# Attention, a dense MLP and a routed MoE on one core: the SP transfer queue follows the written table, and the zero fill of the result becomes eighteen transfers in the first pass

## The chip, the core and the metric

The kernel runs on one core of a Trainium2 chip. The core has a matrix engine (TensorE, PE in the profile), three more compute engines (VectorE or DVE, ScalarE or ACT, GpSimd or POOL) and SyncE (SP), which here only issues transfers. Each engine works through its own list of instructions in order and waits on semaphores; the transfers themselves run on sixteen DMA engines. The metric is the device time of one execution in microseconds (us); of several executions the median is taken.

## The reference

Three layers in float32 precision, one after the other:

```python
# 1 attention: 4 batches x 8 heads, 576 positions, head size 64, window 128
scores = q @ k.T / 8;  scores += -slope[h] * |i - j|  where 0 <= i - j < 128, else -1e9
x = softmax(scores) @ v                       # 2304 tokens x 512
# 2 dense MLP, 512 -> 2048 -> 512
x = (relu(x @ w_in) ** 2) @ w_out
# 3 mixture of experts: 8 experts, 512 -> 1024 -> 512, two per token
noisy = x @ w_gate + log1p(exp(x @ w_noise)) * noise
top2  = two largest per token, weights = softmax over the two
out   = zeros(2304, 512)
for e in range(8): out[mask] += weight * (relu(x[mask] @ w1[e]) @ w2[e])
```

The result starts as zeros because each expert adds its rows to it.

## The kernel before

**Tiling.** The 2304 tokens are 18 tiles of 128. Attention works tile by tile (tile i needs the keys and values of tiles i-1 and i), the dense MLP on 9 groups g of two tiles, with the hidden layer cut into 16 chunks f. To keep float32 precision every operand of a product is split into a high and a low part, and three products are summed (`mm1`, `mm2`, lines 284 to 295).

**Stages.** First pass, to about 160 us: the attention of tiles 0 to 5 and the MLP of groups 0 to 2, while the 32 half chunks of the MLP's weights are loaded and unpacked. From then on one group after the other (groups 3 to 8, some 60 us each), each beside the attention of the next two tiles and the gate of an earlier group. From about 525 us on the experts' weights are loaded, and the experts run to the end; their rows are gathered from the scratch tensor `yd` in HBM and the results scattered into the output.

**What sets the order.** A table `ORDER` of some 1900 steps is written out by hand. A step is a name and indices and calls one small function. The names used below:

- `LQ.i` and `LK.i` load the 512 KB tile `qks` (queries and keys of tile i, line 366), `LV.i` the 256 KB tile `vs` (values, line 370). `LVx` is a second load of the values of tile 5.
- `KH.i`, `KL.i`, `Q1.i`, `QH.i`, `QL.i` scale and split queries and keys (`kth`, `ktl`, `qh`, `ql`); `KHx`, `KLx` do it once more for tile 5. From tile 6 on `Q1` and `QL` run on POOL.
- `AV.i` multiplies probabilities (`pv`, `pc`) with the values of tiles i-1 and i (line 511).
- `H.g.f`, `E1.g.f`, `E2.g.f`, `GL.g.f`, `Y.g.f` are one chunk of the dense MLP: first product (line 290), relu, square and high part on ACT (lines 538, 544, 545), low part on DVE (line 550), second product (line 295).
- `WL.h` loads half chunk h of the MLP's weights (512 KB, line 250); `WA.h` is its first use, on ACT (line 258), and further steps unpack it.
- `YA.g`, `YB.g` copy a finished group to `ysb` and store it in `yd` (line 570); `G5.g` stores the gate weights of a group (`g_wd`, line 664); `TABA`, `TABP`, `TABC` build the experts' token tables (DVE lines 702 to 705 make `r_a` and `r_b`, PE line 713 multiplies them).
- `EL.k` loads chunk k of the experts' weights (`wst`, line 217), `EA.k` and `EB.k` split it.

The table holds for PE, ACT, DVE and POOL. SP is not in the set: its transfers are put in an order by the scheduler of the framework, which takes each when it reckons that it becomes ready.

**Buffers around the change.** From tile 6 on there is one `qks` buffer, so `LQ.6` needs `KLx` done with it, and two `vs` buffers, so `LV.i` needs `AV.(i-1)` done. In the first pass `kth` has seven slots; slot 0 stands for the keys before tile 0, is set to zero once and stays zero.

**The zero fill.** `consts_late` (line 319) runs when the first pass is over. It loads the gate's weights and noise (`wg`, `nz`), clears a tile (line 337) and writes it to all 18 tiles of the result in one transfer (line 338).

Of the kernel before, what the change touches and what calls it, by code (L numbers as in the profile page):

```python
# [50 lines left out]
Y.0.11 WR.27 GL.1.10 E1.2.4 WC.27 E2.2.4 Y.1.10 WB.28 WL.30 WA.29 H.0.12 GL.2.4 WR.28 WG.29 WC.28 Y.2.4 E1.0.12
E2.0.12 WB.29 H.1.11 WL.31 WA.30 GL.0.12 WR.29 WG.30 Y.0.12 E1.1.11 WC.29 E2.1.11 H.2.5 GL.1.11 WB.30 Y.1.11
WA.31 E1.2.5 WG.31 E2.2.5 H.0.13 WR.30 GL.2.5 WC.30 Y.2.5 E1.0.13 WB.31 E2.0.13 H.1.12 GL.0.13 WR.31 WC.31
Y.0.13 E1.1.12 LK.5 E2.1.12 LV.6 H.2.6 LVx.5 GL.1.12 Y.1.12 E1.2.6 E2.2.6 H.0.14 GL.2.6 KHx KLx Y.2.6 E1.0.14
LQ.6 E2.0.14 H.1.13 GL.0.14 Y.0.14 E1.1.13 E2.1.13 H.2.7 Q1.6 KH.6 GL.1.13 KL.6 QH.6 Y.1.13 E1.2.7 QL.6 E2.2.7
# [15 lines left out]
NM.9.1 TY.1.1 XH.8 GL.3.13 H.3.15 QH.10 M.9.0 TYC.1.1 QL.10 E1.3.14 XL.8 TP.9.1 E2.3.14 RANK.0 YB.2 LOG.1 LQ.11
M.9.1 Y.3.13 RANKC.0 AV.9 LOGC.1 GL.3.14 E1.3.15 TABA.0.0 E2.3.15 Q1.11 FOLD.1 LV.10 Y.3.14 XH.9 G1.1 GL.3.15
A1.1 XL.9 TABP.0.0 G2.1 Y.3.15 A2.1 TABA.0.1 H.4.0 TABC.0.0 G3.1 TABP.0.1 H.4.1 E1.4.0 TABC.0.1 E2.4.0 G4.1
H.4.2 GL.4.0 A4.1 Y.4.0 E1.4.1 G5.1 E2.4.1 RANK.1 H.4.3 GL.4.1 E1.4.2 RANKC.1 E2.4.2 Y.4.1 TABA.1.0 H.4.4 GL.4.2
E1.4.3 E2.4.3 Y.4.2 GL.4.3 E1.4.4 E2.4.4 TABP.1.0 Y.4.3 TABA.1.1 H.4.5 GL.4.4 TABC.1.0 TABP.1.1 Y.4.4 E1.4.5
# [5 lines left out]
E1.4.12 E2.4.12 Y.4.11 G5.2 C0.11.1 GL.4.12 EX.11.0 C1.11.1 RANK.2 H.4.13 MX.11.1 KH.12 RS.11.0 Y.4.12 QH.12
RANKC.2 NM.11.0 EX.11.1 H.4.14 TABA.2.0 E1.4.13 E2.4.13 AV.10 RS.11.1 KL.12 NM.11.1 GL.4.13 E1.4.14 QL.12
E2.4.14 TP.11.0 LV.11 TP.11.1 XH.10 GL.4.14 TABP.2.0 LQ.13 M.11.0 Y.4.13 M.11.1 H.4.15 TABA.2.1 AV.11 E1.4.15
E2.4.15 XL.10 Q1.13 TABC.2.0 TABP.2.1 GL.4.15 LV.12 Y.4.14 XH.11 TABC.2.1 XL.11 Y.4.15 H.5.0 H.5.1 E1.5.0 E2.5.0
H.5.2 GL.5.0 E1.5.1 E2.5.1 Y.5.0 GL.5.1 E1.5.2 E2.5.2 Y.5.1 GL.5.2 H.5.3 Y.5.2 E1.5.3 E2.5.3 H.5.4 GL.5.3 Y.5.3
# [1009 lines left out]
```

## Time and profile before

| | before |
|---|---|
| median of 3 runs | 1049.85 us (1049.78 to 1050.63) |
| the profiled execution | 1050.41 us |
| its span, first to last instruction | 1048.6 us |
| mean granted TensorE clock | 0.984 of full speed |
| PE busy | 992.9 us, 95% of the span |
| DVE, ACT, POOL busy | 577.2, 508.5, 245.7 us (55%, 48%, 23%) |
| moved by DMA | 103.40 MB, mean 99 GB/s |

The span is what the profile's rows speak of; the execution's time is 1.8 us longer. PE is busy nearly throughout, so what counts is the idle time in front of its matmuls, and the stretches in which its clock was granted at half speed.

### The profile page before, as it was taken

To read this page: it belongs to the slowest core of one execution; us is meant where nothing else is said; L and a number is where in the kernel's file an instruction comes from. 1 tells how busy PE (TensorE), PEld (TensorE's weight loads), DVE (VectorE), ACT (ScalarE), POOL (GpSimd) and SP (SyncE) were. 2 spreads that over 40 slices of the span, in tenths; PEclk is the share of its full clock that TensorE was granted. 3 is DMA by queue.
4 is the path that set the end of the run, shared out by engine and by line. 5 is a ranking of instruction groups with operands and counts; after the bars stand their busy time and mean duration, and the time that the engine had idled before them with its cause. 6 is when DMAs were issued, how large, how long until landed. Compare 5 with 4: busy or idle time off the path is not lost.

```text
span 1048.6 us, 17826 instructions
## 1 busy us (share of the span) xinstructions
PE 992.9 (95%) x6636; PEld 870.2 (83%) x6636; DVE 577.2 (55%) x1693; ACT 508.5 (48%) x1245; POOL 245.7 (23%) x220
## 2 busy tenths in 40 slices
...
GB/s 280 59 142 103 167 81 260 42 71 22 51 13 31 41 42 41 41 42 13 20 102 152 167 71 228 137 116 177 90 170 117 170 95 170 123 88 68 46 47 48
DMA packets 36234, 103.40 MB, mean 99 GB/s; under 512 B 7495, under 2 KB 7751, under 8 KB 36144
## 3 DMA queue, kind: packets, MB, share of 16 engines
...
HBM read 85.24 MB, written 20.00 MB: 100 GB/s over the span
## 4 chain that ended last, share of the span: by engine, by line
PE 66%; DVE 14%; DMA 8%; issue 5%; ACT 4%; POOL 2%; SPq 1%; POOLq 0%; DVEq 0%; ACTq 0%
PE h L290 30%; PE y L295 29%; DMA old<-out_dram,idx 4%; PE y L421 2%; PE y L511 2%; DMA qks<-in_qk_dram 2%; PE y L798 1%; DVE sb L447 1%; ACT sb L459 1%; DVE gl L550 1%; DMA vs<-in_v_dram 1%; DVE w L280 1%; DVE sb L438 1%; PE y L490 1%; DVE pc L498 1%
## 5 line engine op out<-in xcount | busy, mean ns | idle before, releaser
L290 PE MATMUL h<-xh,w 128*128 128x256 f32 x1152 | 229.7, 285 | 0.0
L290 PE MATMUL h<-xeh,w 128*128 128x304 f32 (+2 forms) x1024 | 229.2, 305 | 0.0
L295 PE MATMUL y<-w,gh 128*128 128x512 f32 x576 | 186.6, 405 | 8.2 <-ACT gh L545 8.2
L290 PEld LDWEIGHTS h<-xh,w 128*128 128x128 f32 x1152 | 187.8, 191 | 7.0 <-issue 1.2
L295 PE MATMUL y<-w,hh 128*128 128x512 f32 (+1 forms) x584 | 182.6, 394 | 0.0
L290 PEld LDWEIGHTS h<-xeh,w 128*128 128x128 f32 x1024 | 171.5, 188 | 2.9 <-issue 0.4
L290 PE MATMUL h<-xl,w 128*128 128x256 f32 x576 | 163.1, 283 | 1.1 <-DVE xl L527 1.0
L290 PE MATMUL h<-xel,w 128*128 128x304 f32 (+2 forms) x512 | 154.8, 302 | 0.3 <-DVE wt L815 0.3
L226 DVE TENSOR_TENSOR w<-wst,w 128x1024 fp32r<-128x1024 f32 x64 | 78.4, 1225 | 138.2 <-ACT w L222 131.6
L550 DVE TENSOR_TENSOR gl<-r,gh 128x256 fp32r<-128x256 f32 x144 | 68.4, 475 | 123.1 <-ACT gh L545 122.9
L222 ACT ACTIVATE w<-wst 128x1024 fp32r<-128x1024 f32 x64 | 67.7, 1058 | 127.9 <-PE y L295 113.0
L295 PEld LDWEIGHTS y<-w,gh 128*128 128x128 f32 x576 | 99.9, 190 | 27.5 <-ACT gh L545 8.4
L295 PEld LDWEIGHTS y<-w,hh 128*128 128x128 f32 (+1 forms) x584 | 103.2, 182 | 21.8
L538 ACT ACTIVATE r<-h 128x256 f32<-128x256 f32 x144 | 54.8, 381 | 136.5 <-PE h L290 96.8
L838 ACT ACTIVATE hh<-h 128x304 fp32r<-128x304 f32 (+1 forms) x118 | 49.7, 421 | 141.5 <-PE h L290 138.0
L295 PE MATMUL y<-w,gl 128*128 128x512 f32 x288 | 114.3, 397 | 1.5 <-DVE gl L550 1.4
L290 PEld LDWEIGHTS h<-xl,w 128*128 128x128 f32 x576 | 110.1, 191 | 5.8 <-DVE xl L527 1.9
L295 PE MATMUL y<-w,hl 128*128 128x512 f32 (+1 forms) x292 | 114.9, 394 | 0.0
L843 DVE SCALAR_TENSOR_TENSOR hl<-h,hh 128x304 fp32r<-128x304 f32 (+1 forms) x118 | 55.0, 467 | 98.2 <-ACT hh L838 91.5
L774 POOL DMA_INDIRECT xg<-yd,idx x40 | 42.4, 1060 | 258.6 <-PE h L290 92.1
L290 PEld LDWEIGHTS h<-xel,w 128*128 128x128 f32 x512 | 96.4, 188 | 2.0 <-DVE wt L815 0.5
L264 POOL TENSOR_SCALAR wsg<-wa 128x512 f32<-128x512 f32 x32 | 54.9, 1717 | 65.3 <-ACT wa L258 52.3
(180 smaller groups left out, 1478.0 us busy)
## 6 DMA issues: line engine op xcount, KB each, us to landing
wst<-in_w_exp_dram SPq DMA_DIRECT2D x64, 512.0 KB, 3.6
w<-in_w_moe_dram SPq DMA_DIRECT2D x32, 512.0 KB, 3.7
qks<-in_qk_dram SPq DMA_DIRECT2D x19, 512.0 KB, 3.6
...
out_dram<-ysb SPq DMA_DIRECT2D x1, 4608.0 KB, 15.3
...
xg<-yd,idx POOLq DMA_INDIRECT x40
out_dram<-old,idx POOLq DMA_INDIRECT x29
```

Source lines behind the costliest of these rows:

```text
L222: nc.scalar.activation(w[:, 0], st, AF.Copy)
L226: nc.vector.tensor_tensor(out=w[:, 1], in0=st, in1=w[:, 0].bitcast(F32), op=OP.subtract)
L264: nc.gpsimd.tensor_scalar(sg.bitcast(F32), a.bitcast(F32), 0.0, None, op0=OP.mult)
L290: nc.tensor.matmul(ps, w[:, wi, c], x[:, kk, :], start=(n == 0), stop=(n == 3 * KD - 1))
L295: nc.tensor.matmul(ps, g, w[:, wi, DM:], start=(start and n == 0), stop=(stop and n == 2))
L421: nc.tensor.matmul(sp[c][:, pp], a[r, p, :], b[r, p, s0:s0 + 2, :], start=(n == 0), stop=(n == 2))
L511: nc.tensor.matmul(o[64 * c:64 * c + 64, 2 * hf + pp, :], vv[n][:, 4 * hf + j, :], pts[n][:, j, :], start=(n == 0), stop=(n == 1))
L538: nc.scalar.activation(r, HT.pop((g, f)), AF.Relu)
L550: nc.vector.tensor_tensor(out=gl, in0=r, in1=gh.bitcast(F32), op=OP.subtract)
L774: nc.gpsimd.indirect_dma_start(out=xg, out_offset=None, in_=yd[:rows, :], in_offset=col(e, t), bounds_check=rows - 1, oob_is_err=False)
L838: nc.scalar.activation(HH[e, f, part][0][:, c0:c1], HP[e, f, part][j], AF.Relu)
L843: nc.vector.scalar_tensor_tensor(out=hl, in0=HP[e, f, part][j], scalar=0.0, in1=hh.bitcast(F32), op0=OP.max, op1=OP.subtract)
```

## The change

1. SP joins the set of engines that follow the table. Its transfers are issued in the order of the steps.
2. The single zero fill is gone, with the tile that it was copied from and that tile's clear on DVE. A new step `ZF.t` writes one tile of 128 rows of the result (256 KB) from slot 0 of `kth`. That slot is four runs of 128 floats in each partition, so one step writes 512 runs of 512 bytes. The table has eighteen: four after `WL.5`, four after `WL.6`, and one after each of `WL.7` to `WL.16`.
3. The loads of `wg` and `nz` become a step `LR`, after `LQ.6`.
4. The copies of the token weights of experts 0 and 1 (`wt`) need no longer keep the written place. On DVE they stay where they were.

PE, ACT and POOL have the same instructions in the same order as before, DVE too but for the clear that is gone. The diff (of the table one line of each):

```diff
-EX.0.1 RS.0.0 MX.1.0 NM.0.0 LQ.5 KH.4 MX.1.1 EX.1.0 RS.0.1 WC.0 TP.0.0 EX.1.1 WB.2 S.2.0 RS.1.0 WG.3 WL.5 C0.2.0
+NM.0.0 LQ.5 KH.4 MX.1.1 EX.1.0 RS.0.1 WC.0 TP.0.0 EX.1.1 WB.2 S.2.0 RS.1.0 WG.3 WL.5 ZF.3 ZF.2 ZF.1 ZF.0 C0.2.0
...
         nc.vector.memset(runcum, 0.0)
+
+    def l_rout():
         nc.sync.dma_start(out=wg.rearrange("p k e -> p (k e)"), in_=w_gate)
         nc.sync.dma_start(out=nz.rearrange("p t e -> p (t e)"), in_=noise)
-        z = gp.tile([P, DM], F32, name="ysb", bufs=2)
-        nc.vector.memset(z, 0.0)
-        nc.sync.dma_start(out=out.rearrange("(t p) d -> p t d", p=P),
-                          in_=z[:, None, :].to_broadcast([P, NTILE, DM]))
+
+
+    def z_rows(t):
+        nc.sync.dma_start(out=out[t * P:(t + 1) * P, :].rearrange("p (a b) -> p a b", b=P),
+                          in_=A["kt"][0][:, :, 0, :].bitcast(F32))
...
-        tc.keep_in_program_order(nc.vector.tensor_copy(WT[e][:, t:t + 1], xg[:, DM + e:DM + e + 1]))
+        wt = nc.vector.tensor_copy(WT[e][:, t:t + 1], xg[:, DM + e:DM + e + 1])
+        if e > 1:
+            tc.keep_in_program_order(wt)
...
-    order = {mybir.EngineType.PE, mybir.EngineType.Activation, mybir.EngineType.DVE, mybir.EngineType.Pool}
+    order = {mybir.EngineType.PE, mybir.EngineType.Activation, mybir.EngineType.DVE, mybir.EngineType.Pool,
+             mybir.EngineType.SP}
```

On SP at the end of the first pass, before (a row is the line, the transfer's destination and source, and the shape; `qks` is `LK.5`, then `LQ.6` and `LQ.7`, `vs` is `LV.6` and `LVx`):

```order
L366 DMA qks<-in_qk_dram 128x1024
L370 DMA vs<-in_v_dram 128x512
L338 DMA out_dram<-ysb 128x18x512
L370 DMA vs<-in_v_dram 128x512
L366 DMA qks<-in_qk_dram 128x1024 x2
L570 DMA yd<-ysb 128x512 x2
```

The same place on SP now:

```order
L367 DMA qks<-in_qk_dram 128x1024
L371 DMA vs<-in_v_dram 128x512 x2
L367 DMA qks<-in_qk_dram 128x1024
L334 DMA wg<-in_w_gate_dram 128x128
L335 DMA nz<-in_noise_dram 128x144
L367 DMA qks<-in_qk_dram 128x1024
L571 DMA yd<-ysb 128x512 x2
```

The large store that stood ahead of `LVx`, `LQ.6` and `LQ.7` is gone, and the two small loads of the gate stand between `LQ.6` and `LQ.7`.

On SP at the turn from one group to the next, before (`g_wd` is `G5.2`, `qks` is `LQ.13`, `vs` is `LV.11` and `LV.12`, then `LQ.14`):

```order
L664 DMA yd<-g_wd 128x2x8
L366 DMA qks<-in_qk_dram 128x1024
L370 DMA vs<-in_v_dram 128x512 x2
L366 DMA qks<-in_qk_dram 128x1024
L570 DMA yd<-ysb 128x512 x2
```

The same place on SP now:

```order
L665 DMA yd<-g_wd 128x2x8
L371 DMA vs<-in_v_dram 128x512
L367 DMA qks<-in_qk_dram 128x1024
L371 DMA vs<-in_v_dram 128x512
L367 DMA qks<-in_qk_dram 128x1024
L571 DMA yd<-ysb 128x512 x2
```

`LV.11` has moved ahead of `LQ.13`. It is the same for `LV.13` and `LV.15` in the two groups that follow.

On SP in the first pass now, from `WL.5` on (before, the `w` rows stood there alone, with the same neighbours; `out_dram<-kth` is `ZF`):

```order
L248 DMA w_366<-in_w_moe_dram 128x1024
L339 DMA out_dram<-kth 512x1x128 x4
L248 DMA w_461<-in_w_moe_dram 128x1024
L339 DMA out_dram<-kth 512x1x128 x4
L248 DMA w_689<-in_w_moe_dram 128x1024
L339 DMA out_dram<-kth 512x1x128
L248 DMA w_735<-in_w_moe_dram 128x1024
L339 DMA out_dram<-kth 512x1x128
```

Each `ZF` stands behind a load of weights and ahead of the next one.

## Rows read from the trace of the kernel before

**Rows 1.** Waits of PE, 180 us to the end: us in total, times, longest.

```profile
PE y L295 <- ACT gh L545: 8.2, 1, 8.2
PE y L511 <- DMA vs<-in_v_dram: 4.7, 3, 1.6
```

**Rows 2.** Timeline of SP's queue at 155 to 166.5 us: start, us.

```profile
159.72 0.40 SPq L338 DMA_DIRECT2D out_dram<-ysb  x1
160.17 6.33 SPq L370 DMA_DIRECT2D vs<-in_v_dram  x1
```

**Rows 3.** Timeline of all engines at 156 to 182 us: [idle before <-releaser].

```profile
162.68 0.69 DVE L386 TENSOR_TENSOR ktl<-qks,kth 128x512 fp32r<-128x512 f32 x1
...
167.33 0.42 ACT L545 ACTIVATE gh<-r 128x256 fp32r<-128x256 f32 x1
...
171.80 0.28 PE L290 MATMUL h<-xh,w 128*128 128x256 f32 x1
177.23 0.63 ACT L382 ACTIVATE kth<-qks 128x512 fp32r<-128x512 f32 x1 [9.48 <-DMA qks<-in_qk_dram]
```

**Rows 4.** Chain that ended last, 0 to 450 us: start, us, what.

```profile
180.26 2.93 PE y L295 x6
183.19 2.37 PE h L290 x12
185.56 1.40 PE y L295 x6
186.96 1.41 PE h L290 x12
```

**Rows 5.** DMA issues of the page: KB each, median us to landing.

```profile
qks<-in_qk_dram SPq DMA_DIRECT2D x19, 512.0 KB, 3.6
...
out_dram<-ysb SPq DMA_DIRECT2D x1, 4608.0 KB, 15.3
```

**Rows 6.** Stretches: busy of each engine, PEclk, DMA share, GB/s.

```profile
0.00:20.00 20.00, 5.83 (x48) 4.95 (x48) 14.84 (x60) 12.40 (x29) 5.07 (x8) 0.95 0.88 321
...
159.70:166.00 6.30, 6.30 (x44) 5.76 (x43) 1.77 (x4) 2.96 (x7) 0.00 (x0) 1.00 1.03 396
...
175.00:178.00 3.00, 0.00 (x0) 0.00 (x0) 0.11 (x1) 0.63 (x1) 0.67 (x1) 0.50 0.34 137
...
508.50:511.50 3.00, 3.00 (x30) 2.62 (x29) 2.79 (x18) 1.96 (x7) 0.00 (x0) 1.00 0.05 3
```

**Rows 7.** Timeline, first pass: issues of WL.5, WL.7, WL.17, and WA.7.

```profile
27.21 0.33 SPq L250 DMA_DIRECT2D w<-in_w_moe_dram  x1
...
49.72 0.33 SPq L250 DMA_DIRECT2D w<-in_w_moe_dram  x1
...
53.57 0.67 ACT L258 ACTIVATE wa<-w 128x512 f32<-128x512 f32 x1 [0.21 <-DMA w<-in_w_moe_dram]
...
88.35 0.33 SPq L250 DMA_DIRECT2D w<-in_w_moe_dram  x1
```

**Rows 8.** Timeline of all engines at 337 to 348 us.

```profile
337.18 0.39 PE L511 MATMUL y<-pc,vs 128*64 128x128 f32 x4
...
340.69 0.33 SPq L366 DMA_DIRECT2D qks<-in_qk_dram  x1
...
344.40 1.12 POOL L378 TENSOR_TENSOR qks<-qks,qscale 128x512 f32<-128x512 f32 x1 [3.74 <-DMA qks<-in_qk_dram]
344.54 1.07 DVE L703 TENSOR_SCALAR r_b<-io,r_rf 128x152 bf16<-128x152 f32 x1
...
345.53 0.35 DVE L705 TENSOR_SCALAR r_b<-io,r_rf,pid 128x152 bf16<-128x152 f32 x1
...
346.60 0.43 PE L713 MATMUL y<-r_b,r_a 128*128 128x304 bf16 x2
```

**Rows 9.** Timeline around EL.4, at 540 to 565 us.

```profile
550.95 0.38 SPq L664 DMA_DIRECT2D yd<-g_wd  x1
...
556.31 0.38 ACT L538 ACTIVATE r<-h 128x256 f32<-128x256 f32 x1 [1.39 <-PE y L713]
```

More of the change, by code (lines that the diff above doesn't have):

```diff
@@ L51 @@
[L51 to L55, printed above, removed]
@@ L71 @@
[L71 to L75, printed above, removed]
@@ L81 @@
[L81 to L85, printed above, removed]
@@ new lines @@
+GL.1.1 QL.4 E1.0.3 WG.10 E2.0.3 Y.1.1 Q1.5 WR.8 WB.9 QH.5 H.1.2 GL.0.3 WR.9 WL.12 ZF.13 WC.8 WA.11 Y.0.3 KL.5
+E1.1.2 WG.11 WC.9 E2.1.2 QL.5 H.0.4 GL.1.2 WB.10 Y.1.2 E1.0.4 WL.13 ZF.14 E2.0.4 WB.11 S.4.0 WR.10 WA.12 GL.0.4
+H.1.3 WR.11 WC.10 WG.12 C0.4.0 WC.11 Y.0.4 C1.4.0 E1.1.3 WL.14 ZF.15 E2.1.3 MX.4.0 S.4.1 WA.13 GL.1.3 EX.4.0 WB.12
+WG.13 H.0.5 C0.4.1 RS.4.0 Y.1.3 NM.4.0 E1.0.5 WL.15 ZF.16 E2.0.5 C1.4.1 H.1.4 WR.12 MX.4.1 WA.14 GL.0.5 EX.4.1
+WG.14 S.5.0 WC.12 WB.13 Y.0.5 C0.5.0 WL.16 ZF.17 E1.1.4 RS.4.1 C1.5.0 E2.1.4 H.0.6 NM.4.1 MX.5.0 WR.13 WA.15 S.5.1
@@ new lines @@
+H.2.4 GL.0.11 E1.1.10 WG.28 E2.1.10 Y.0.11 WR.27 GL.1.10 E1.2.4 WC.27 E2.2.4 Y.1.10 WB.28 WL.30 WA.29 H.0.12 GL.2.4
+WR.28 WG.29 WC.28 Y.2.4 E1.0.12 E2.0.12 WB.29 H.1.11 WL.31 WA.30 GL.0.12 WR.29 WG.30 Y.0.12 E1.1.11 WC.29 E2.1.11
+H.2.5 GL.1.11 WB.30 Y.1.11 WA.31 E1.2.5 WG.31 E2.2.5 H.0.13 WR.30 GL.2.5 WC.30 Y.2.5 E1.0.13 WB.31 E2.0.13 H.1.12
+GL.0.13 WR.31 WC.31 Y.0.13 E1.1.12 LK.5 E2.1.12 LV.6 H.2.6 LVx.5 GL.1.12 Y.1.12 E1.2.6 E2.2.6 H.0.14 GL.2.6 KHx KLx
+Y.2.6 E1.0.14 LQ.6 LR E2.0.14 H.1.13 GL.0.14 Y.0.14 E1.1.13 E2.1.13 H.2.7 Q1.6 KH.6 GL.1.13 KL.6 QH.6 Y.1.13 E1.2.7
@@ new lines @@
+QH.10 M.9.0 TYC.1.1 QL.10 E1.3.14 XL.8 TP.9.1 E2.3.14 RANK.0 YB.2 LOG.1 LQ.11 M.9.1 Y.3.13 RANKC.0 AV.9 LOGC.1
+GL.3.14 E1.3.15 TABA.0.0 E2.3.15 Q1.11 FOLD.1 LV.10 Y.3.14 XH.9 G1.1 GL.3.15 A1.1 XL.9 TABP.0.0 G2.1 Y.3.15 A2.1
+TABA.0.1 H.4.0 TABC.0.0 G3.1 TABP.0.1 H.4.1 E1.4.0 TABC.0.1 E2.4.0 G4.1 H.4.2 GL.4.0 A4.1 Y.4.0 E1.4.1 G5.1 E2.4.1
+RANK.1 H.4.3 GL.4.1 E1.4.2 RANKC.1 E2.4.2 Y.4.1 TABA.1.0 H.4.4 GL.4.2 E1.4.3 E2.4.3 Y.4.2 GL.4.3 E1.4.4 E2.4.4
+TABP.1.0 Y.4.3 TABA.1.1 H.4.5 GL.4.4 TABC.1.0 TABP.1.1 Y.4.4 E1.4.5 TABC.1.1 E2.4.5 GL.4.5 S.10.0 H.4.6 C0.10.0
@@ new lines @@
+C1.10.0 Y.4.5 MX.10.0 E1.4.6 E2.4.6 S.10.1 EX.10.0 GL.4.6 H.4.7 KH.11 RS.10.0 QH.11 NM.10.0 KL.11 Y.4.6 C0.10.1
+E1.4.7 QL.11 C1.10.1 E2.4.7 H.4.8 MX.10.1 LQ.12 TY.2.0 GL.4.7 EX.10.1 TY.2.1 YB.3 Y.4.7 TYC.2.0 RS.10.1 TYC.2.1
+H.4.9 NM.10.1 E1.4.8 E2.4.8 Q1.12 LOG.2 YA.3 GL.4.8 H.4.10 E1.4.9 LOGC.2 E2.4.9 GL.4.9 FOLD.2 E1.4.10 Y.4.8 E2.4.10
+G1.2 A1.2 GL.4.10 Y.4.9 G2.2 A2.2 H.4.11 G3.2 TP.10.0 E1.4.11 G4.2 S.11.0 E2.4.11 M.10.0 TP.10.1 A4.2 Y.4.10
+GL.4.11 M.10.1 C0.11.0 H.4.12 C1.11.0 MX.11.0 S.11.1 E1.4.12 E2.4.12 Y.4.11 G5.2 C0.11.1 GL.4.12 EX.11.0 C1.11.1
@@ new lines @@
+RANK.2 H.4.13 MX.11.1 KH.12 RS.11.0 Y.4.12 QH.12 RANKC.2 NM.11.0 EX.11.1 H.4.14 TABA.2.0 E1.4.13 E2.4.13 AV.10
+RS.11.1 KL.12 NM.11.1 GL.4.13 E1.4.14 QL.12 E2.4.14 TP.11.0 LV.11 TP.11.1 XH.10 GL.4.14 TABP.2.0 LQ.13 M.11.0
+Y.4.13 M.11.1 H.4.15 TABA.2.1 AV.11 E1.4.15 E2.4.15 XL.10 Q1.13 TABC.2.0 TABP.2.1 GL.4.15 LV.12 Y.4.14 XH.11
+TABC.2.1 XL.11 Y.4.15 H.5.0 H.5.1 E1.5.0 E2.5.0 H.5.2 GL.5.0 E1.5.1 E2.5.1 Y.5.0 GL.5.1 E1.5.2 E2.5.2 Y.5.1 GL.5.2
+H.5.3 Y.5.2 E1.5.3 E2.5.3 H.5.4 GL.5.3 Y.5.3 E1.5.4 E2.5.4 H.5.5 GL.5.4 S.12.0 E1.5.5 E2.5.5 Y.5.4 C0.12.0 GL.5.5
@@ new lines @@
+C1.13.1 H.5.13 MX.13.1 KH.14 H.5.14 QH.14 RS.13.0 EX.13.1 GL.5.12 NM.13.0 TABA.3.0 Y.5.12 E1.5.13 RS.13.1 E2.5.13
+KL.14 AV.12 NM.13.1 GL.5.13 E1.5.14 QL.14 E2.5.14 TP.13.0 LV.13 XH.12 GL.5.14 TP.13.1 LQ.15 M.13.0 TABP.3.0 Y.5.13
+M.13.1 H.5.15 TABA.3.1 AV.13 E1.5.15 Q1.15 XL.12 E2.5.15 TABC.3.0 GL.5.15 TABP.3.1 LV.14 Y.5.14 XH.13 TABC.3.1
+XL.13 Y.5.15 H.6.0 H.6.1 E1.6.0 E2.6.0 H.6.2 GL.6.0 E1.6.1 E2.6.1 Y.6.0 GL.6.1 E1.6.2 E2.6.2 Y.6.1 GL.6.2 H.6.3
+Y.6.2 E1.6.3 E2.6.3 H.6.4 GL.6.3 Y.6.3 E1.6.4 E2.6.4 H.6.5 GL.6.4 S.14.0 E1.6.5 E2.6.5 Y.6.4 C0.14.0 GL.6.5 C1.14.0
@@ L132 @@
-EB.17 TX.1.1 TA.1.0 X2.1.2 TA.1.1 TB.1.0 EV.1.3 XG.1.2 EL.19 X1.1.4 TB.1.1 EA.18 XG.1.3 X2.1.3 EB.18 EH.1.4
-EV.1.4 X1.1.5 EL.20 EA.19 X2.1.4 EH.1.5 EB.19 TX.1.2 EV.1.5 TX.1.3 TA.1.2 X1.1.6 TA.1.3 TB.1.2 EL.21 EA.20
-TB.1.3 XG.1.4 X2.1.5 EH.1.6 EB.20 X1.1.7 EV.1.6 X2.1.6 EH.1.7 EL.22 EA.21 EV.1.7 EB.21 TX.1.4 TA.1.4 EA.22
-TB.1.4 EB.22
+AV.14 NM.15.1 GL.6.13 E1.6.14 QL.16 E2.6.14 TP.15.0 LV.15 XH.14 GL.6.14 TP.15.1 LQ.17 M.15.0 TABP.4.0 Y.6.13 M.15.1
+H.6.15 TABA.4.1 AV.15 E1.6.15 Q1.17 XL.14 E2.6.15 TABC.4.0 GL.6.15 TABP.4.1 LV.16 Y.6.14 XH.15 TABC.4.1 XL.15
@@ new lines @@
+G3.5 E2.7.10 H.7.11 GL.7.10 G4.5 TP.16.0 E1.7.11 S.17.0 E2.7.11 M.16.0 TP.16.1 A4.5 Y.7.10 GL.7.11 M.16.1 C0.17.0
+H.7.12 G5.5 C1.17.0 S.17.1 MX.17.0 E1.7.12 E2.7.12 RANK.5 TY.6.0 RANKC.5 C0.17.1 Y.7.11 EX.17.0 C1.17.1 H.7.13
+MX.17.1 TYC.6.0 RS.17.0 TY.6.1 EX.17.1 GL.7.12 AV.16 NM.17.0 TABA.5.0 TYC.6.1 RS.17.1 E1.7.13 TP.17.0 LV.17 NM.17.1
+E2.7.13 LOG.6 M.17.0 XH.16 Y.7.12 LOGC.6 GL.7.13 TP.17.1 XL.16 TABP.5.0 H.7.14 M.17.1 TABA.5.1 H.7.15 E1.7.14
+E2.7.14 TABC.5.0 FOLD.6 GL.7.14 AV.17 E1.7.15 G1.6 E2.7.15 A1.6 GL.7.15 G2.6 TABP.5.1 A2.6 Y.7.13 XM.0 EL.0
@@ new lines @@
+TABC.5.1 XM.1 XH.17 Y.7.14 G3.6 Y.7.15 XL.17 G4.6 EL.1 H.8.0 A4.6 YB.7 H.8.1 E1.8.0 G5.6 YA.7 E2.8.0 TY.7.0 TY.7.1
+GL.8.0 TYC.7.0 H.8.2 TYC.7.1 E1.8.1 E2.8.1 Y.8.0 GL.8.1 E1.8.2 LOG.7 E2.8.2 Y.8.1 EA.0 LOGC.7 GL.8.2 EB.0 FOLD.7
+EA.1 H.8.3 G1.7 EL.2 EB.1 A1.7 Y.8.2 E1.8.3 G2.7 E2.8.3 RANK.6 A2.7 H.8.4 GL.8.3 RANKC.6 EL.3 EA.2 Y.8.3 G3.7
+E1.8.4 E2.8.4 G4.7 H.8.5 TABA.6.0 A4.7 H.8.6 GL.8.4 EA.3 EB.2 TABP.6.0 Y.8.4 E1.8.5 G5.7 EL.4 E2.8.5 TABA.6.1
+RANK.7 H.8.7 GL.8.5 E1.8.6 RANKC.7 TABP.6.1 E2.8.6 Y.8.5 TABA.7.0 EA.4 H.8.8 GL.8.6 E1.8.7 TABC.6.1 E2.8.7 TABP.7.0
@@ new lines @@
+EB.3 Y.8.6 TABA.7.1 EL.5 H.8.9 GL.8.7 E1.8.8 EB.4 TABP.7.1 E2.8.8 Y.8.7 TABC.7.1 GL.8.8 EL.6 EP EA.5 TABC.6.0
+H.8.10 ED E1.8.9 E2.8.9 Y.8.8 EB.5 XG.0.0 GL.8.9 H.8.11 E1.8.10 TABC.7.0 XG.0.1 EL.7 E2.8.10 Y.8.9 EA.6 GL.8.10
+E1.8.11 EB.6 H.8.12 E2.8.11 GL.8.11 EL.8 EA.7 Y.8.10 E1.8.12 EB.7 E2.8.12 H.8.13 GL.8.12 Y.8.11 E1.8.13 E2.8.13
+EL.9 H.8.14 EA.8 GL.8.13 EB.8 TX.0.0 E1.8.14 TX.0.1 E2.8.14 Y.8.12 TA.0.0 EL.10 GL.8.14 TA.0.1 TB.0.0 H.8.15 EA.9
+TB.0.1 XG.0.2 EB.9 Y.8.13 E1.8.15 E2.8.15 Y.8.14 EL.11 EA.10 GL.8.15 EB.10 Y.8.15 TX.0.2 YA.8 YB.8 TA.0.2 EL.12
```

148 lines of the change are left out of this document (59 added, 89 removed).

## The prediction

> **What bounds the kernel now.** I started with the waits of PE, since PE is busy for 95% of the span and only what stands in front of its matmuls can give time back. After 180 us two waits stand out: 8.2 us, once, for a high part `gh` from ACT, and 4.7 us in three pieces for values `vs` from DMA [rows 1]. Both lead to SP's queue. Next I read that queue at the end of the first pass: the zero fill is issued at 159.72, and the small load behind it, `LVx`, is held in the queue for 6.33 us [rows 2], although the fill's own issue took 0.40. So `LVx` is out of the queue at 160.17 + 6.33 = 166.5 and `LQ.6` goes only after it; ACT gets that tile at 177.23 [rows 3], 10.7 us later, where such a load has a median of 3.6 [rows 5]: the fill, issued at 159.72 and 15.3 us in flight [rows 5], is ahead of it until 175.0. Between 159.7 and 166 the DMA engines are full, at 396 GB/s [rows 6]. Then the timeline of all engines: ACT sits idle for 9.48 us before `KH.6` at 177.23, by name for `qks` [rows 3]. `KH.6` stands in ACT's list ahead of `E1.2.7`, whose `gh` PE needs for `Y.2.7`; PE's last matmul starts at 171.80 [rows 3] and its next at 180.26 [rows 4]. The wait for `gh` is thus the zero fill's, three engines further on. The clock follows: 0.50 granted between 175 and 178 [rows 6], that is 1.2 GHz after PE had stood still, and the first six and twelve matmuls after the gap take 2.93 and 2.37 us where the next such pieces take 1.40 and 1.41 [rows 4].
>
> **Part 1: the fill leaves the end of the first pass.** `LQ.6` then waits for `KLx`, which ends at 162.68 + 0.69 = 163.4 [rows 3], and lands 3.6 later [rows 5], at 167.0. ACT is free at 167.33 + 0.42 = 167.75 [rows 3], so its order decides and not the load. What is late next: POOL's scaling (1.12 us for the same instruction in [rows 8]) ends at 168.2, `KH.6` and `QH.6` on ACT at 0.63 each [rows 3] end at about 169.0, `E1.2.7` and the two instructions of `E2.2.7` at 0.42 [rows 3] at about 170.3. PE asks at 171.80 + 0.28 = 172.1. The cover is 1.8 us; a load later than 168.8 would cost PE what it is later. I take the whole gap: 8.2 us [rows 1], and with it the slow restart, (2.93 - 1.40) + (2.37 - 1.41) = 2.5 us [rows 4]. Together **10.7 us**. All engines stood still there, so everything behind moves up with PE. `wg` and `nz` now stand behind `LQ.6`, before `LQ.7`, and are wanted a group later: nothing. The clear on DVE stood in a stretch in which DVE was busy for 1.77 of 6.30 us [rows 6]: nothing.
>
> **Part 2: the values ahead of the queries.** `AV.11` needs `LV.11`. That load could go when `AV.10` is over, at 337.18 + 0.39 = 337.6, but stands behind `LQ.13`, issued at 340.69 [rows 8]; `LQ.13` waits for POOL to be done with the buffer. Now it goes behind `LQ.13`, at 340.69 + 0.33 = 341.0 at the earliest; moved ahead, at about 337.7, some 3.3 us sooner. The longest of the waits is 1.6 us: the wait on `vs` goes, three times, 4.7 us in all [rows 1]. But PE meets the next wait soon: right behind `AV.11` stands `TABP`, and its last operand `r_b` is ready at 345.53 + 0.35 = 345.9, while PE gets there at 346.60 [rows 8]. Without the wait PE would be there at 345.0 and stand until 345.9. What is left is 0.65 us; with three like places **2.0 us**, between 0 and the full 4.7. It is so late because of a clash: DVE's `r_b` of 344.54 takes 1.07 us, while the like instruction behind it takes 0.35, and POOL's `Q1` begins at 344.40 [rows 8]; that hangs on `LQ.13`, which goes no earlier than before.
> The Trainium skill, "SBUF — State Buffer", section "Who interferes with whom", says that DVE and GpSimd share a pair of ports that one of them holds for a whole instruction, the other being blocked fully. By that rule the clash stays wherever `Q1` meets `r_b`, and the part is worth 2.0; were the 1.07 chance, it would be up to 4.7. The trace agrees with the rule in that DVE's instruction ends (345.61) just after POOL's (345.52).
>
> **Part 3: eighteen stores in the first pass.** 18 x 512 = 9,216 runs of 512 bytes, 576 for each DMA engine. The trace has no such store. From below: the gate's store writes 256 runs of 32 bytes, alone at 508.5 to 511.5; share 0.05 x 16 engines x 3.0 us / 256 = 9.4 ns a run [rows 6]. From above: the fill's runs of 2048 bytes at 396 GB/s [rows 6], 24.75 GB/s an engine, are 83 ns. By bytes at that rate 512 are 20.7 ns; I add the 9.4 and take 30, or 1.0 us of all engines for a store. A 512 KB load is 1.3 us at that rate. The first eight stores lie between `WL.5` at 27.21 and `WL.7` at 49.72 [rows 7]: 8 x 1.0 + 2 x 1.3 = 10.6 of 22.5 us. From there ten loads go out until 88.35 [rows 7], one in 3.9 us: 1.0 + 1.3 = 2.3 of 3.9. The sums fit, and no store holds anything that an engine waits for: **0**. If that cover is gone, the place is `WL.7`: ACT already waits 0.21 us for it at 53.57 [rows 7]. At 83 ns the eight stores take 8 x 2.66 + 2.6 = 23.9 of 22.5, 1.4 us late there, and 2.66 + 1.3 = 3.96 of 3.9 after it: some 2 us late in all. No gain is possible, since nothing there waits for what left. The buffer that `kth` gives up later waits for the last store, long done by then.
> The Trainium skill, "DMA: Bandwidth & Descriptors", section "Bandwidth", speaks against this: transfers are to be batched to 1 MiB or more, since each has a fixed part of some 2.0 us beside bytes / 436 GB/s. By it a pair of a 256 KB store and a 512 KB load would take 2.6 + 3.2 = 5.8 us in place of the 3.9, if one is served after the other: 1.9 us late for each of ten pairs, 19 us in all, an estimate from that page, and the sum would be a loss. It is rival D below. No row here shows 256 KB stores queued behind one another.
>
> **Part 4: SP in written order.** Some loads now stand behind a store. The closest is `EL.4`, which stood ahead of `g_wd` and now goes behind it, at 550.95 + 0.38 = 551.3 [rows 9], an estimated 1.3 us later than before (its own issue, the one of `g_wd` and the wait between them). ACT unpacks it, and is idle for 1.39 us before its instruction at 556.31 [rows 9]; that takes the delay up. Without that cover up to 1.3 is lost. Three others (`LQ.9`, `LQ.11`, `EL.12`) go a like time later, and PE's waits name nothing that they feed: **0**, up to 1.3 lost.
>
> **Sum.** 10.7 + 2.0 + 0 + 0 = 12.7 us. The profiled execution took 1050.41, its span 1048.6; after the change I expect a span of 1035.9. The runs' median is 0.56 below the profiled time, so the forecast is 1049.85 - 12.7 = **1037.1 us**.
>
> **The rivals.**
> - A. The clash on `r_b` falls otherwise and the waits on `vs` give all of their 4.7: 1034.4. For it: where a transfer lands by a few tenths decides who blocks whom. Against: `Q1` hangs on `LQ.13`, and this on POOL, neither of which moves against PE's neighbours.
> - B. Part 1 is right, and 2 to 5 us come back: the stores 2, the order 1.3, part 2 nothing instead of 2.0: up to 1042.4. For it: `WL.7` and `EL.4` have next to no slack.
> - C. The change doesn't do what it says: `LQ.6` is held by something other than the fill (its buffer, or POOL), PE still stands for some 10 us, and part 2 alone remains: 1047.9. Against: the queue itself shows 6.33 us for an issue, and ACT was waiting for that one load.
> - D. Slower. The first pass serves store and load one after the other at their full time to landing, so that `WL.8` to `WL.17` come in a row, each late. At 3.6 us for a load [rows 5] and by bytes half of that, 1.8, for a store, 5.4 against 3.9: 1.5 us late ten times, 15 us, and 1049.85 - 12.7 + 15 = 1052.2. It decides against the change from 3.9 + 1.27 = 5.2 us a pair. Against it: in the first 20 us loads on the same queue overlap to 321 GB/s [rows 6], which one transfer of 512 KB in 3.6 us, 146 GB/s, could not reach.
>
> **How the numbers follow.** The forecast's own range, 1035.5 to 1039, 0.62; A 0.11; B 0.18; C 0.04; D 0.05. Down to A and up to B's end the range is 1034 to 1042.5, with 0.09 outside it. About 0.2% (2.1 us) is what a measurement of this kernel can tell from no change: faster 0.91, same 0.04 (C), slower 0.05 (D).
>
> **What would show it.** Part 1: no row of SP's queue above 1 us after `LK.5`, `LQ.6` issued within 6 us of `LK.5`, no idle of ACT on `qks` there, clock 1.00 throughout 160 to 200. Part 2: `PE y L511 <- DMA vs` gone, a wait on `r_b` of 0.5 to 0.9 us behind `AV.11`, `AV.13` and `AV.15`. Part 3: no wait of `wa` on DMA of more than a few tenths, the first pass over at the same time, a store's runs near 30 ns. Part 4: no new wait on `wst`. Wrong would be: PE still idle for several us near 172, or the end of the first pass, `KLx` on DVE at 162.68 [rows 3], more than 2 us later.

## The result: 1037.2 us where 1050.2 stood

In runs taken side by side on one chip the changed kernel has a median of 1037.16 us (1036.56 to 1037.3, 4 runs), the kernel before one of 1050.24 (1049.78 to 1053.71, 4 runs): a ratio of 0.9867, 95% interval 0.9846 to 0.9889. The forecast was 1037.1. The span of the profiled execution fell from 1048.6 to 1035.5 us. Its mean granted clock is 0.997 where 0.984 stood, but not all of that belongs to the change: the other three executions of the changed kernel have 0.987 to 0.995 and take as long (1036.56 to 1037.3 us).

Waits of PE from 180 us on, after the change (us in total, times, longest), the counterpart of [rows 1]:

```profile
PE y L714 <- DVE r_b L706: 4.2, 8, 0.8
PE y L491 <- POOL sb L484: 1.1, 1, 1.1
PE y L799 <- DMA xg<-yd,idx: 1.1, 1, 1.1
```

Both rows of before are gone: the 8.2 us on `gh` and the 4.7 us on `vs`. In the place of the second the wait on `r_b` has grown; before it was this:

```profile
PE y L713 <- DVE r_b L705: 1.8, 5, 0.6
```

SP's queue at the end of the first pass, after (start, us), the counterpart of [rows 2]:

```profile
158.06 0.33 SPq L367 DMA_DIRECT2D qks<-in_qk_dram  x1
158.44 1.84 SPq L371 DMA_DIRECT2D vs<-in_v_dram  x2
163.69 0.33 SPq L367 DMA_DIRECT2D qks<-in_qk_dram  x1
164.12 0.38 SPq L334 DMA_DIRECT2D wg<-in_w_gate_dram  x1
164.54 0.42 SPq L335 DMA_DIRECT2D nz<-in_noise_dram  x1
```

`LQ.6` goes 5.6 us behind `LK.5`, as soon as `KLx` has ended (162.97 + 0.69). The same moment on the other engines, all engines at 167 to 174 us (in brackets the idle time before and what ended it), against [rows 3]:

```profile
167.41 1.04 POOL L379 TENSOR_TENSOR qks<-qks,qscale 128x512 f32<-128x512 f32 x1 [8.73 <-DMA qks<-in_qk_dram]
...
167.95 0.62 ACT L383 ACTIVATE kth<-qks 128x512 fp32r<-128x512 f32 x1
...
169.59 0.38 ACT L539 ACTIVATE r<-h 128x256 f32<-128x256 f32 x1 [0.47 <-PE h L288]
...
170.45 0.42 ACT L546 ACTIVATE gh<-r 128x256 fp32r<-128x256 f32 x1
...
172.21 0.63 PE L293 MATMUL y<-w,gh 128*128 128x512 f32 x2
```

POOL starts when the tile has landed, at 167.41. `KH.6` (167.95) has no idle time before it any more; `E1.2.7` at 169.59 even waits 0.47 us for PE's own product. Its `gh` is ready at 170.87, PE uses it at 172.21: 1.3 us of cover.

Stretches after the change, against [rows 6] (length, busy time of PE, PEld, DVE, ACT, POOL, granted clock, DMA share, GB/s):

```profile
27.20:34.00 6.80, 5.70 (x39) 4.54 (x40) 6.45 (x22) 4.94 (x17) 4.34 (x6) 1.00 0.84 235
34.00:50.00 16.00, 12.39 (x118) 10.74 (x115) 14.74 (x56) 14.45 (x56) 5.17 (x6) 0.89 0.36 99
50.00:90.00 40.00, 38.89 (x301) 33.20 (x301) 38.79 (x86) 30.58 (x78) 17.69 (x12) 1.00 0.71 199
...
160.00:200.00 40.00, 39.71 (x270) 34.97 (x269) 16.03 (x51) 23.68 (x67) 8.48 (x7) 1.00 0.25 78
```

At the granted clock of 1.00, 2.4 GHz, PE is busy for 39.71 of the 40 us from 160 on. The first three stretches, where the eighteen stores now are, looked like this before:

```profile
27.20:34.00 6.80, 5.70 (x39) 4.54 (x40) 6.44 (x22) 4.95 (x17) 4.34 (x6) 0.50 0.28 81
34.00:50.00 16.00, 12.39 (x121) 10.78 (x118) 14.74 (x56) 14.76 (x57) 5.41 (x6) 0.86 0.10 34
50.00:90.00 40.00, 38.89 (x303) 33.09 (x301) 39.10 (x88) 30.66 (x77) 17.87 (x12) 1.00 0.44 135
```

The share of the transfer engines rose from 0.28, 0.10 and 0.44 to 0.84, 0.36 and 0.71, and PE's busy times did not move. The clock column of 27.20:34.00 (0.50 before, 1.00 after) is no effect of the change: PE is busy for the same 5.70 us in both, and the trace of the changed kernel has no record of the clock before 35.5 us.

**Where the time came from.** In both traces `E1` begins 144 times, and its starts cut the run into stretches that can be compared step by step (us, from the timelines; the kernels below the first two are the experiments of the next section; `E1.1.13` is the last before the old gap, `E1.1.15` is beyond it, `E1.4.15` to `E1.7.0` holds the three places of `vs`):

```
                       start of   to       to       to      to       start of
                       E1.1.13  E1.1.15  E1.4.15  E1.7.0  E1.8.15  E1.8.15
before                  166.46   24.76   151.84   127.82  106.63    577.51
after                   166.76   14.08   151.78   125.32  106.63    564.57
v_behind_q              166.84   14.08   151.75   127.70  106.63    567.00
one_fill_in_order       166.50   24.81   151.81   125.31  106.65    575.08
stores_after_pass       166.70   14.08   151.79   125.34  106.63    564.54
sp_by_scheduler         165.66   14.08   151.85   127.91  106.63    566.13
q_later                 166.95   14.08   151.78   122.97  106.62    562.40
four_large_at_wl5       167.56   14.09   151.68   125.39  106.60    565.32
fill_behind_lq7         166.89   21.46   154.01   125.25  106.60    574.21
four_large_behind_lq7   166.06   14.09   151.77   125.40  106.62    563.94
stores_twice            191.41   14.08   151.79   125.27  106.60    589.15
stores_twice_apart      166.88   14.08   151.78   125.28  106.65    564.67
```

From before to after the gap gives 24.76 - 14.08 = 10.7 us and the three places 127.82 - 125.32 = 2.5; the first pass ends 0.3 later. The rest, from `E1.8.15` to the end of the span, is 471.1 us before and 470.9 after, and 469.9 to 471.8 in the twelve traces, whatever the edit. A stretch between two marks that an edit does not touch repeats to 0.2 us, so the table resolves more than the medians do, whose runs lie up to 4.2 us apart.

### The profile page after: what moved, and what is told of

Read it like the earlier page. It is cut to its first block, busy times and chain, and to the rows that moved or that the text cites. A ratio compares the mean times of both kernels' runs of the same rounds, so it can differ in the third digit from the quotient of the medians.

```text
span 1035.5 us, 17850 instructions
## 1 busy us (share of the span) xinstructions
PE 991.6 (96%) x6636; PEld 869.3 (84%) x6636; DVE 576.8 (56%) x1692; ACT 507.9 (49%) x1245; POOL 243.2 (23%) x220
## 4 chain that ended last, share of the span: by engine, by line
PE 66%; DVE 17%; DMA 7%; issue 5%; ACT 4%; POOL 1%; SPq 0%; POOLq 0%; DVEq 0%; ACTq 0%
PE h L288 30%; PE y L293 30%; DMA old<-out_dram,idx 4%; PE y L422 2%; DVE gl L551 2%; DVE sb L448 1%; PE y L799 1%; DVE pc L499 1%; DVE pv L498 1%; ACT sb L460 1%; DVE sb L439 1%; PE y L512 1%; DVE w L278 1%; PE y L491 1%; DVE w L267 1%
```

## The experiments

Each kernel is the changed one but for the edit shown.

**v_behind_q: the values behind the queries again.**

```diff
-LV.11 ... TABP.2.0 LQ.13 M.11.0
+... TABP.2.0 LQ.13 LV.11 M.11.0
```

The same for `LV.13` behind `LQ.15` and `LV.15` behind `LQ.17`.

> The changed kernel with one thing undone: LV.11, LV.13 and LV.15 stand behind LQ.13, LQ.15 and LQ.17 again, as before the change; the eighteen stores stay. Theory (the order of values and queries gives its own part of the gain, limited by r_b): the three waits of PE on vs come back with 4.7 us, the waits on r_b fall from 4.2 to about 1.8, and the time is 1037.2 + 2.4 = 1039.6. Rival (the whole gain is the fill's place; the values' order only swaps one wait for another of the same size): 1037.2 within 0.5. Rival (the full 4.7 was gained there): 1041.9.

Measured: 1040.59 us (1038.25 to 1041.76, 6 runs), 1.0 above what was expected, with runs 3.5 us apart. PE's waits from 180 us on:

```profile
PE y L512 <- DMA vs<-in_v_dram: 4.5, 3, 1.6
PE y L714 <- DVE r_b L706: 1.8, 5, 0.6
```

The one wait is traded for the other, 4.5 for 4.2 - 1.8 = 2.4, and the three places take 127.70 us again, 2.4 more than in the changed kernel. The median alone would not tell the theory from the second rival; the waits and the three places do, and neither rival holds: the order of the values is worth half of the wait that it removes.

**one_fill_in_order: one transfer at the old place, SP by the table.**

```diff
-WL.5 ZF.3 ZF.2 ZF.1 ZF.0 ...
+LV.6 H.2.6 ZF.0 LVx.5
```

The two lines stand at different places of the table. The one step writes a cleared `ysb` tile to all 18 tiles; the other `ZF` are gone.

> The changed kernel with the zero fill again as one transfer of 4608 KB from a cleared tile, between LV.6 and LVx at the end of the first pass; SP follows the table. Theory (the fill's size and place, ahead of LQ.6, is what PE stood still for): ACT waits some 9.5 us for LQ.6, PE some 8 us for gh, the restart costs 2.5, and the first pass ends 0.3 us sooner for lack of the stores: 1037.2 + 10.7 - 0.3 = 1047.6. Rival (the order written for SP is what freed LQ.6, whatever the fill does): 1037 to 1039.

Measured: 1048.03 us (1046.49 to 1049.36, 9 runs), and PE's longest wait is back:

```profile
PE y L293 <- ACT gh L546: 8.2, 1, 8.2
```

SP's queue there:

```profile
159.75 0.40 SPq L340 DMA_DIRECT2D out_dram<-ysb  x1
160.20 5.95 SPq L371 DMA_DIRECT2D vs<-in_v_dram  x1
166.24 1.20 SPq L367 DMA_DIRECT2D qks<-in_qk_dram  x1
```

The load behind the fill is held for 5.95 us, and the gap is back in full (24.81 in the table), while the three places keep their gain. The two parts of the change are independent and add up.

**stores_after_pass: the same stores later.**

```diff
-WL.5 ZF.3 ZF.2 ZF.1 ZF.0 ...
+Y.2.8 ZF.0 ... Y.3.9 ZF.17
```

Their source is the table `tab`, which is zero until group 4.

> The changed kernel with the same eighteen stores of 256 KB, but none of them in the first pass: one behind each of Y.2.8 to Y.2.15 and Y.3.0 to Y.3.9 (source: a table that is still zero there, read in runs of 512 bytes as before). Theory (in the first pass the stores lie in gaps of the transfer engines and cost next to nothing): 1036.9, at most 0.3 below the changed kernel, which is what its first pass ends later than that of the kernel before. Rival (each store holds the load behind it, rival D in small): 1035.5 or less, with the first pass over 1 us or more sooner.

Measured: 1038.13 us (1035.07 to 1038.44, 5 runs), `E1.1.13` at 166.70. The median is 1.2 above what was expected; `E1.8.15` starts where it does in the changed kernel (564.54 and 564.57), and the difference lies behind it, where no store stands (471.8 us to the end in place of 470.9). Without any store the first pass is over no sooner than with all eighteen (166.76). So the stores cost it nothing that shows. The 0.3 us that I had put on them is not theirs: the traces of all kernels but `stores_twice` reach this point between 165.66 and 167.56, and part of the scatter is there at 8.3 us, when no store has been issued. `KH` of the second tile, changed kernel first, then the next experiment:

```profile
8.33 0.63 ACT L383 ACTIVATE kth<-qks 128x512 fp32r<-128x512 f32 x1 [1.86 <-DMA qks<-in_qk_dram]
```

```profile
7.95 0.63 ACT L383 ACTIVATE kth<-qks 128x512 fp32r<-128x512 f32 x1 [1.56 <-DMA qks<-in_qk_dram]
```

**sp_by_scheduler: SP out of the set.**

```diff
-    order = {..., mybir.EngineType.Pool, mybir.EngineType.SP}
+    order = {..., mybir.EngineType.Pool}
```

> The changed kernel with SP out of the set that follows the table: the scheduler orders its transfers. It puts the values behind the queries again (three places), and sends all eighteen stores before WL.8: six before WL.5, six behind it, six behind WL.6, none after. Theory (the two parts add up, and the loads of the first pass have slack where the stores now stand): 1039.6 by the values' order, up to 1 us more if LQ.5 or WL.5 come late. Rival (without the written order the gain of the fill is lost too): 1047 to 1050. Rival (the written order costs or gives nothing): 1037.2.

Measured: 1039.39 us (1037.99 to 1040.12, 5 runs); the wait on `vs` is back with 4.6 us. The three places take 127.91 us, the gap stays gone. The first pass ends 1.1 us sooner, of which 0.4 stood already at 8.3 us (rows above); that the earlier stores help is not shown. The written order is worth the 127.91 - 125.32 = 2.6 us of the three places, and costs nothing that shows.

**q_later: the query load and its scaling on POOL behind the values that follow.**

```diff
-TABP.2.0 LQ.13 ... XL.10 Q1.13 ... GL.4.15 LV.12
+TABP.2.0 ... XL.10 ... GL.4.15 LV.12 LQ.13 Q1.13
```

The same for 15 and 17.

> The changed kernel with LQ.13, LQ.15 and LQ.17 moved behind LV.12, LV.14 and LV.16, each with its Q1 on POOL behind it. The load then goes some 4 us later, POOL's Q1 begins at about 338.4 in place of 333.9, and DVE's r_a and r_b are done by then. Theory (the 0.8 us wait on r_b that is left in three places is the clash of POOL's Q1 with DVE's r_a or r_b): no DVE instruction of these lines above 0.4 us, the waits on r_b fall from 4.2 to about 1.8, and the time is 1037.2 - 2.4 = 1034.8. Rival (r_b is late for its own chain on DVE, whatever POOL does): 1037.2. Rival (the clash moves on to TABC or the low parts of x, which PE waits for as well): 1037 to 1039.

Measured: 1034.96 us (1033.32 to 1035.58, 5 runs), a ratio of 0.985 to the kernel before (0.9835 to 0.9866). First the place in the changed kernel, then the same place here:

```profile
333.93 1.15 POOL L379 TENSOR_TENSOR qks<-qks,qscale 128x512 f32<-128x512 f32 x1 [3.71 <-DMA qks<-in_qk_dram]
...
334.10 1.08 DVE L704 TENSOR_SCALAR r_b<-io,r_rf 128x152 bf16<-128x152 f32 x1
...
335.10 0.35 DVE L706 TENSOR_SCALAR r_b<-io,r_rf,pid 128x152 bf16<-128x152 f32 x1
...
335.50 0.29 PE L714 MATMUL y<-r_b,r_a 128*128 128x304 bf16 x1 [0.79 <-DVE r_b L706]
```

```profile
334.28 0.29 DVE L704 TENSOR_SCALAR r_b<-io,r_rf 128x152 bf16<-128x152 f32 x1
...
334.49 0.35 DVE L706 TENSOR_SCALAR r_b<-io,r_rf,pid 128x152 bf16<-128x152 f32 x1
...
334.60 0.58 PE L714 MATMUL y<-r_b,r_a 128*128 128x304 bf16 x2
...
338.78 1.04 POOL L379 TENSOR_TENSOR qks<-qks,qscale 128x512 f32<-128x512 f32 x1 [8.37 <-DMA qks<-in_qk_dram]
```

PE's wait on `r_b` here, 180 us to the end:

```profile
PE y L714 <- DVE r_b L706: 1.8, 5, 0.6
```

With POOL silent the same DVE instruction takes 0.29 us in place of 1.08, PE's two products run back to back, and the three places take 122.97 us: 2.35 less than after, 4.85 less than before. The clash was the limit and not `r_b`'s own chain. This kernel is faster than the changed one too: its slowest run is ahead of that one's fastest (1036.56).

**four_large_at_wl5: the same runs in four transfers.**

```diff
-WL.5 ZF.3 ZF.2 ZF.1 ZF.0 ...
+WL.5 ZF.0 ZF.1 ZF.2 ZF.3
```

Each step writes 128 columns of all 18 tiles, 1152 KB; the other fourteen `ZF` are gone.

> The changed kernel with the same 9216 runs of 512 bytes in four transfers of 1152 KB, all behind WL.5, in place of eighteen of 256 KB. Theory (only the bytes and the place count): 9216 runs at 27 ns over 16 engines are 15.6 us from 27.6, so WL.6, which is issued at about 34, lands at about 44.5; its first use is at 47.5, nothing waits, 1037.2 within 1. Rival (few large transfers are served better, as by the Trainium skill, DMA: Bandwidth & Descriptors, section Bandwidth; 18 x 2.0 us of fixed cost are saved): the loads of the first pass land sooner and the time is 1036 or less. Rival (a long transfer holds the queue as at the end of the first pass before): WL.6 or WL.7 late by 5 us and PE with it, 1041 or more.

Measured: 1037.14 us (1036.92 to 1037.83, 4 runs), the changed kernel's time to 0.02 us. SP:

```profile
27.71 12.36 SPq L339 DMA_DIRECT2D out_dram<-kth  x4
40.17 10.81 SPq L248 DMA_DIRECT2D w<-in_w_moe_dram  x2
```

SP is held over the four for 12.36 us, `WL.6` goes at 40.17 in place of 34.08, and ACT's first use of it, at 47.9 us with the one before it, has no idle time in front of it that shows. `E1.1.13` comes at 167.56, 0.8 us later than in the changed kernel, but 0.7 of that stands at 42 us already, before this use; the two medians agree more closely than the scatter allows one to read. Within that scatter, neither the number of transfers nor the gap between them matters here. The Trainium skill, "DMA: Bandwidth & Descriptors", section "Anatomy of one DMA — SWDGE (gpsimd) path", has a fixed part of some 2.0 us for each transfer, from a fit to transfers that GpSimd issues (the section "Bandwidth", which the prediction names for it, has the rule on 1 MiB). Fourteen transfers fewer would be 28 us of it, an estimate from that page, if they were served one after the other; these are issued by SP, and this run shows no such saving.

**fill_behind_lq7, four_large_behind_lq7: all of it at one place later.**

```diff
-WL.5 ZF.3 ZF.2 ZF.1 ZF.0 ...
+LQ.7 ZF.0
```

One transfer of 4608 KB from a cleared `ysb` tile; and in the second kernel, as four of 1152 KB with the table `tab` as source:

```diff
-WL.5 ZF.3 ZF.2 ZF.1 ZF.0 ...
+LQ.7 ZF.0 ZF.1 ZF.2 ZF.3
```

In both the `ZF` of the first pass are gone.

> The changed kernel with the fill again as one transfer of 4608 KB from a cleared tile, but behind LQ.7, where the next things in the queue are stores of a finished group. Theory (not the size of the fill but the load that stood behind it cost the time): no wait of PE on gh, 1037.2 within 1. Rival (a transfer of 4608 KB costs PE some us wherever it stands, since it fills all transfer engines for 12 us or more): 1040 to 1048.

> As the fill of 4608 KB behind LQ.7, which held the ysb buffer that DVE's copy of a finished group needs, but in four transfers of 1152 KB from a table that is still zero there, so that no ysb buffer is held; no store in the first pass. Theory (the 9.4 us lost with the fill behind LQ.7 were its source buffer, not its traffic): DVE does not wait for the fill, PE has no wait of 6.9 us on gl, and the time is 1037.2 within 1. Rival (so much traffic at once costs PE wherever it stands: the stores of the finished group behind it, held in the queue, are what DVE and PE wait for): 1041 to 1047.

Measured: 1046.55 us (1046.12 to 1047.01, 5 runs) and 1037.1 (1036.5 to 1037.28, 4 runs). My theory fell in the first, which lost 9.4 us. Its trace:

```profile
177.13 11.13 SPq L571 DMA_DIRECT2D yd<-ysb  x2
187.23 0.69 DVE L569 COPY ysb<-y 128x512 f32<-128x512 f32 x1 [10.15 <-DMA out_dram<-ysb]
188.31 0.79 PE L293 MATMUL y<-w,gl 128*128 128x512 f32 x1 [6.91 <-DVE gl L551]
```

DVE waits 10.15 us for the fill, because the fill still reads one of the two `ysb` buffers that a finished group is copied into; `gl` stands behind that copy, and PE waits for it. The second kernel, with a source that nobody wants, tells traffic from buffer (it also splits the fill in four; the wait that goes is the one that names the buffer). SP's queue, and the stretch in which the transfers run:

```profile
170.33 12.33 SPq L339 DMA_DIRECT2D out_dram<-tab  x4
182.70 3.75 SPq L571 DMA_DIRECT2D yd<-ysb  x2
```

```profile
170.00:190.00 20.00, 20.00 (x141) 17.47 (x140) 7.72 (x26) 11.66 (x34) 3.58 (x3) 1.00 0.98 290
```

The transfer engines are full (0.98) for 20 us, the stores of the finished group stand behind the fill, and PE is busy for 20.00 of 20.00. Here the traffic costs nothing where nothing urgent is behind it; the load behind it cost 10.7 us, its source buffer 9.4.

**stores_twice, stores_twice_apart: thirty-six stores.**

```diff
     def z_rows(t):
         nc.sync.dma_start(out=out[t * P:(t + 1) * P, :]..., in_=A["kt"][0]...)
+        nc.sync.dma_start(out=out[t * P:(t + 1) * P, :]..., in_=A["kt"][0]...)
```

```diff
     def z_rows(t):
-        nc.sync.dma_start(out=out[t * P:(t + 1) * P, :]..., in_=A["kt"][0]...)
+        for u in (t, (t + 9) % NTILE):
+            nc.sync.dma_start(out=out[u * P:(u + 1) * P, :]..., in_=A["kt"][0]...)
```

> The changed kernel with every one of the eighteen stores issued twice. Theory (a store is 512 runs of 27 ns over 16 engines, 0.86 us; twice that and a load of 1.3 us are 3.0 of 3.9 us): WA.7 and WA.9 wait up to 1 us longer, PE hardly, 1037.2 to 1038.2. Rival (rival D: a store holds the load behind it for a full time to landing of some 2 us): 36 stores where 18 are 15 us worse or more, 1045 to 1060.

> The changed kernel with thirty-six stores in place of eighteen at the same places, each step writing tile t and tile t + 9 (modulo 18), so that no two stores to the same rows stand next to each other; in the run before, the second store to the same rows was held in the queue until the first had landed, some 4 us for each. Theory (without that wait a store costs its 512 runs of 27 ns over 16 engines, 0.86 us, and 2 x 0.86 + 1.3 are 3.0 of the 3.9 us that a load has): the loads of the first pass land up to 1 us later each, PE loses 0 to 2 us, 1037.2 to 1039. Rival (rival D: it is the number of transfers on the queue that costs, each some 2 us): 1050 or more.

Measured: 1060.95 us (1060.63 to 1062.1, 5 runs) and 1037.61 (1037.12 to 1037.93, 4 runs). By its time alone the first looks like rival D. What SP waits for at the second store of a pair in the first kernel (us in total, times, longest), then SP's queue there, then in the second, and a stretch of the second:

```profile
SPq L341 <- DMA out_dram<-kth: 63.2, 18, 5.7
```

```profile
27.57 0.65 SPq L339 DMA_DIRECT2D out_dram<-kth  x1
32.06 0.54 SPq L341 DMA_DIRECT2D out_dram<-kth  x1
32.65 1.07 SPq L339 DMA_DIRECT2D out_dram<-kth  x1
35.78 0.53 SPq L341 DMA_DIRECT2D out_dram<-kth  x1
...
43.38 0.63 SPq L248 DMA_DIRECT2D w<-in_w_moe_dram  x1
```

```profile
27.63 7.57 SPq L339 DMA_DIRECT2D out_dram<-kth  x8
35.30 0.59 SPq L248 DMA_DIRECT2D w<-in_w_moe_dram  x1
```

```profile
50.00:90.00 40.00, 38.93 (x300) 33.28 (x301) 38.71 (x87) 30.61 (x78) 17.55 (x12) 1.00 0.89 264
```

In the first the second store to the same rows (line 341) waits in the queue until the first has landed, and the loads with it: `WL.6` goes at 43.38 and the first pass ends 25 us late. In the second no two neighbours write the same rows; twice the stores bring the transfer engines to 0.89 of the time, and the first pass ends at 166.88. Up to there the number of stores costs nothing that stands out of the scatter. Waits on a landing are what rival D priced; eighteen of them cost 24 us here, more than its 15, but they come from two stores to the same rows, which the change does not have.

## Why the prediction was right

- **The sum.** The mechanisms came out as forecast. That the median lies within 0.1 us of the forecast is in part luck: part 2 was 0.5 too small, the kernel before stood at 1050.24 in this comparison where the forecast started from 1049.85, and single runs of one kernel lie 0.7 to 4.2 us apart.
- **Part 1, the gap, 10.7 us.** Measured 24.76 - 14.08 = 10.68. The chain of before named the fill, the load behind it, `KH.6` and `gh`; `one_fill_in_order` brings all of it back by the fill alone. The estimates of the steps were 0.2 to 0.6 us early (`KH.6` at 167.95 for 167.75, `gh` for PE at 170.87 for 170.3), and the cover 1.3 us for 1.8: `E1.2.7` waited for PE, not for the load, and so the load could have come 0.47 us later still. One sign that I named did not come out: the two values' loads behind `LK.5` hold the queue for 1.84 us, not under 1.
- **Part 2, the values, 2.0 us.** Measured 2.5 by the marks and 2.4 by `v_behind_q`. The mechanism was right, and the term was too small by 0.1 to 0.2 us in each place: the wait on `r_b` that remains is 0.78 to 0.80 us, where the waits that went were 1.5 to 1.65. Part of it is a slip: 346.60 - 345.88 of the prediction's own rows is 0.72, not 0.65. That the rest is POOL's clash with DVE was an argument from durations then; `q_later` shows it, and 4.85 us is what rival A would have given. The Trainium skill, "SBUF — State Buffer", section "Who interferes with whom", has the engine that comes second blocked fully while the other holds the shared ports for its whole instruction. The trace agrees: DVE's 334.10 + 1.08 = 335.18 ends just behind POOL's 333.93 + 1.15 = 335.08. In the third place POOL met `r_a` instead of `r_b`, for the same 0.8.
- **Part 3, the stores, 0.** Right: `stores_after_pass` ends the first pass at the same time. From the stretches the stores took 16 x (0.56 x 6.8 + 0.26 x 16 + 0.27 x 40) = 300 us of one engine, 33 ns a run (the records of the single runs have a median of 27); I had taken 30. The first uses of `WL.7` and `WL.9` waited 0.39 and 0.54 us for their loads, and PE's busy time from 50 to 90 us is 38.89 in both kernels.
- **Part 4, SP in written order, 0.** `EL.4` went 1.3 us later than at its old place, when the 12.9 us gained by then are taken off (538.48 for 550.07 in the timelines), as estimated, and its use on ACT with it; PE did not notice (106.63 us for the last stretch in both).
- **What I had not seen.** That the fill's source matters as much as its place. I read the change as a matter of the queue; the `ysb` tile of the old fill made one later place nearly as bad as the old one (9.4 us). The zero slot of `kth` is needed by nobody; that this is part of why the new place is free is argued from that run, since none took a wanted buffer as the source in the first pass.
